# Weight conversions at other steps of the attention, and a combination with one ScalarE copy

## The chip, the cores and the metric

The kernel runs on one core of a Trainium2 chip. The metric is the time of one execution on the device in microseconds; it is the median of three runs. Beside it stands one execution that the hardware profiler recorded, with its trace.

## What is computed

Two batches of eight heads attend over 768 positions, each query only to keys in the same hash bucket. The output, as 1536 rows of 512, goes through two expert layers. All of it is float32; matrix products run as sums of a high and a low part of each operand.

```python
q_bits = (np.einsum('bhsd,dk->bhsk', q, proj) > 0)          # 6 bits; k_bits likewise
mask = q_bucket[:, :, :, None] == k_bucket[:, :, None, :]
scores = np.where(mask, scale * np.matmul(q, k.transpose(0, 1, 3, 2)), -1000000000.0)
attn = np.exp(scores - np.max(scores, axis=-1, keepdims=True))
attn = attn / (np.sum(attn, axis=-1, keepdims=True) + 1e-09)
x = np.matmul(attn, v)                                      # to (1536, 512)
h = x @ w_in; g = np.where(h > 0.0, h, np.exp(np.minimum(h, 0.0)) - 1.0); x = g @ w_out
p = domain_probs / (domain_probs.sum(-1, keepdims=True) + 1e-09)
out = sum(p[:, e:e + 1] * (np.maximum(x @ w1[e], 0.0) @ w2[e]) for e in range(4))
```

The weights `w_in` and `w_out` arrive as 64-bit floats and are turned into 32-bit ones on the chip, by integer and float instructions on their two words.

## The kernel before

**Attention.** The sixteen heads go in eight pairs, each pair in twelve steps: six blocks of 128 queries for each of its two heads. The order on every engine is the order in which the program emits its instructions, and in a step (`att_step`) that is the order of the letters in `ORDER`. C combines a finished product with v (`emit_comb`). E is the exponential of the next block (ScalarE), T and t are transposes of its two halves (TensorE), H and h their high parts copied from PSUM (ScalarE, line 431), Q the scores two blocks ahead (TensorE, lines 385 and 386), N their masked minimum (VectorE, line 395), L and l the low parts (VectorE, line 428), M, m and d the preparation of later pairs, V a third of a product with v. The scores have one buffer, so Q waits for the N before it. The step with index 3 of a pair (5 in pair zero) is the hashing step: twelve more products, whose sign VectorE compares on line 371 and SyncE then moves to the operands.

**The combination.** A product with v has its two parts (with the high and with the low part of v) in the two halves of the partitions. Lines 457 and 458 copy them from PSUM by ScalarE, each 64x384, the second into the first one's partitions, and GpSimd adds them on line 459. It runs at every third step. At steps 3 and 6 GpSimd also normalises half of the pair before (`emit_fin`, line 489) and splits it.

**Weight conversion.** `conv_w` turns one block of 128 hidden units of both weights from 64 to 32 bits. In two halves each: an absolute value by ScalarE (line 248), five steps by VectorE (lines 249, 250, 252, 254, 255) and an addition by GpSimd (line 262). Then `consumed` frees the buffer `raw`, of which there is one until step 83 of 96, and queues the load of the next block on SyncE; `split_w` makes the high and low parts on GpSimd. That is a list of eighteen entries per block, for the blocks 0, 1 and 2. It is worked off one entry at a time at the ends of steps 3, 4, 5, 7, 8 and 9 of pairs one to three (block 0) and four to six (block 1), and one or two per step in pair seven (block 2).

**SyncE's queue.** `loads_step` sends the transfers of the next pair at the ends of steps: the placing of q and k and of their bits, sixteen transfers at steps 2 and 3, and the loads of k at step 2 and of q at step 4 for the pair after.

**Probabilities.** `emit_probs` normalises `domain_probs` after step 10 of pair zero: three additions and three more instructions on VectorE.

After the attention come the expert layers, `TAIL` and then long runs of TensorE products.

Of the kernel before, what the change touches and what calls it, by code (L numbers as in the profile page):

```python
# [7 lines left out]
F32 = mybir.dt.float32  # L8
# [4 lines left out]
ACTF = mybir.ActivationFunctionType  # L13
ALU = mybir.AluOpType
PSUM = bass.MemoryType.PSUM

P = 128
# [18 lines left out]
def lsh_attention_moe_kernel(  # L36
# [14 lines left out]
    nc = tc.nc  # L51
    B, H, S, D = q.shape
# [3 lines left out]
    E = dprobs.shape[1]  # L56
# [3 lines left out]
    HS = S // 2  # L60
# [6 lines left out]
    NPRE = 2  # L67
# [3 lines left out]
    assert len(FT) == DFF // P and GS[0] == NPRE + 1  # L71
    NG = G1 + E
    WA = 3
    ORDER = "CETHQtNLhlMmdV"
    WARM = (9, 2, 5)
    GL = 0.0
    TAIL = "AoqpBpcpproppqppVVVncxkgogkqffzkffppppfffffffffffffffffoqfffffffff"
# [9 lines left out]
    cv_p = ctx.enter_context(tc.tile_pool(name="cv", bufs=1))  # L87
# [7 lines left out]
    l1 = late.enter_context(tc.tile_pool(name="l1", bufs=1))  # L95
# [33 lines left out]
    def split_v(g2, par):  # L129
        if par == 0:  # L130
            vs_t[g2] = l2.tile([P, NJ, 4 * D], F32R, tag="vs", name="vs")
        t = vs_t[g2]
        pool_split(t[:, :, 3 * par * D:(3 * par + 1) * D], t[:, :, (1 + par) * D:(2 + par) * D],
                   raws.pop((g2, par)))
# [12 lines left out]
    dp = l1.tile([P, B * NJ, E], F32, tag="rx", name="dp")  # L147
# [28 lines left out]

    def emit_probs():
        sm = edge_t[:, 0:B * NJ]
        nc.vector.tensor_add(sm, dp[:, :, 0], dp[:, :, 1])
        for e in range(2, E):  # L180
            nc.vector.tensor_add(sm, sm, dp[:, :, e])
        nc.vector.tensor_scalar(out=sm, in0=sm, scalar1=1e-9, scalar2=None, op0=ALU.add)
        nc.vector.reciprocal(out=sm, in_=sm)
        nc.vector.tensor_tensor(out=pn, in0=dp, in1=sm.unsqueeze(2).to_broadcast([P, B * NJ, E]),
                                op=ALU.mult)
# [21 lines left out]
    def consumed(g, m, split):  # L207
        if (not split) if wide and g < G1 else (split and m % 2):
            raw_free.append(raw_used.pop(0))
            loads()  # L210
# [54 lines left out]
    def split_w(g, m, pool, eng, part=None):  # L265
        if part != 1:
            wt[g, m] = pool.tile([P, 4, DM], F32R, tag="w", name="w")
        t = wt[g, m]
        for i, s in enumerate(w32[g, m]):
            if part == 1 - i:  # L270
                continue
            hi, lo = t[:, 2 * i, :], t[:, 2 * i + 1, :]
            if i == 0:
                hi = hi.rearrange("p (c f) -> p c f", f=P)
                lo = lo.rearrange("p (c f) -> p c f", f=P)
            if "p" in eng:
                nc.gpsimd.tensor_scalar(out=hi, in0=s, scalar1=1.0, scalar2=1.0, op0=ALU.mult, op1=ALU.mult)
            else:
                nc.scalar.activation(out=hi, in_=s, func=ACTF.Copy)
            if "P" in eng:  # L280
                nc.gpsimd.tensor_tensor(out=lo, in0=s, in1=hi.bitcast(F32), op=ALU.subtract)
            else:
                nc.vector.tensor_tensor(out=lo, in0=s, in1=hi.bitcast(F32), op=ALU.subtract)
        if part != 0:
            del w32[g, m]
# [3 lines left out]
    NU = NPAIR * 2 * NJ  # L289
    UC = NJ // 2  # L290
# [98 lines left out]
    def emit_min(u):  # L389
        mn = a2.tile([P, 1], F32, tag="mn", name="mn")  # L390
        mn_t[u] = mn
        n = u % (3 + EX) if u < NU - PU - EU else (u + (3 + EX) * PU) % 3
        pool, tag = (a4, f"mk{n}") if n < 3 else (xp, "x" + "hl"[n - 3] + str(NC - 1))
# [53 lines left out]
    def emit_comb(c):  # L447
        g, half = divmod(c, 2)
        g2, par = divmod(g, 2)
        if par == 0 and half == 0:  # L450
            u_t[g2] = l2.tile([P, S], F32, tag="u", name="u")
        ps = pv_t.pop(c)
        del pth_t[c], ptl_t[c]
        o0 = par * D
        t1 = l1.tile([P, HS], F32, tag="t1", name="t1")[o0:o0 + D]
        uu = u_t[g2][o0:o0 + D, half * HS:(half + 1) * HS]
        nc.scalar.activation(out=uu, in_=ps[o0:o0 + D, 0:HS], func=ACTF.Copy)
        nc.scalar.activation(out=t1, in_=ps[D - o0:2 * D - o0, 0:HS], func=ACTF.Copy)
        nc.gpsimd.tensor_tensor(out=uu, in0=uu, in1=t1, op=ALU.add)

    def emit_rinv(g2):
        sm = sums_t[g2]
# [38 lines left out]
            nc.tensor.transpose(ps[:, i * P:(i + 1) * P], rx_t[g2][:, half * UC + i].rearrange("p h d -> p (h d)"), ident)  # L501

    PU = 2 * NJ
    M_AT = (0, 1, 2, 3, 10, 11)
    PLACE_AT = (2, 3, 3, 11)
    V_AT = (8, 9)
# [2 lines left out]
    LE, LN, LQ = 1, 2, 2  # L509
    EX = 0  # L510
    EU = 0
    PRE_EVERY = 3
    LASTN = (1, 2, 2, 1, 2, 1, 2, 2, 2, 1, 1, 1)
    FIN_AT = (3, 6)
    PRE_AT = (3, 4, 5, 7, 8, 9)
    MSTEP = [None] * PU
    for i, st in zip(M_AT, (("n",), ("t", "q", 0), ("t", "q", UC), ("h",), ("t", "k", 0), ("t", "k", UC))):
        MSTEP[i] = st
# [14 lines left out]
    def loads_step(g2, i):  # L533
        if g2 + 2 < NPAIR and i in L_AT:
            load_qk(g2 + 2, "kq"[L_AT.index(i)])
        if g2 + 1 < NPAIR:
            q0, b0, kq1, _ = (4, 5, 5, 0) if g2 == 0 else PLACE_AT
            if g2 == 0 and i == 1:
                place(g2 + 1, "k", 0)
            if i == q0:  # L540
                place(g2 + 1, "q", 0)
            if i == b0:
                for nm in "kq":
                    place_bits(g2 + 1, nm, 0)
            if i == kq1:
                for nm in "kq":
                    place(g2 + 1, nm, 1)
                    place_bits(g2 + 1, nm, 1)
        if i == PLACE_AT[3] and g2 + 2 < NPAIR:
            place(g2 + 2, "k", 0)  # L550
        if i in FIN_AT and 0 < g2 < NPAIR:
            half = FIN_AT.index(i)
            emit_fin(g2 - 1, half, rx_t[g2 - 1][:, half * HS:(half + 1) * HS])
        if g2 + 1 < NPAIR and i < 2:
            load_v(g2 + 1, i)
        if g2 + 1 < NPAIR and i in V_AT:
            split_v(g2 + 1, V_AT.index(i))

    def run(stages):
        for f in stages:  # L560
# [68 lines left out]
    for par in range(2):  # L629
        split_v(0, par)  # L630
    nc.sync.dma_start(out=dp.rearrange("p (b j) e -> p b j e", b=B),
                      in_=dprobs.rearrange("(b p j) e -> p b j e", b=B, j=NJ))
# [4 lines left out]
            emit_min(u)  # L637
    for u in range(LE):
        emit_exp(u)
    pre, done = [], []  # L640

    def att_step(u):
        g2, i = divmod(u, PU)
        v = u - LT
        c, part = divmod(v, UC)
        mc[0] = c - 1
        ops = {}
        if u + LQ < NU:
            ops["Q"] = lambda: emit_qk(u + LQ)
        if u + LN < NU:  # L650
            ops["N"] = lambda: emit_min(u + LN)
        if u + LE < NU:
            ops["E"] = lambda: emit_exp(u + LE)
        if done:
            ops["C"] = lambda: emit_comb(done.pop())
        if 0 <= v < NU:
            for h in range(2):
                ops["Tt"[h]] = lambda h=h: emit_t(v, h)
                ops["Hh"[h]] = lambda h=h: emit_parts(v, h, False)
                ops["Ll"[h]] = lambda h=h: emit_parts(v, h, True)  # L660
        if 1 <= c <= NU // UC:
            ops["V"] = lambda: emit_pv(c - 1, part)
        if 1 <= g2 < NPAIR and i == 0:
            emit_rinv(g2 - 1)
        table = MSTEP if g2 else MSTEP0 + [x if x and x[:2] == ("t", "k") else None for x in MSTEP[6:]]
        if g2 == NPAIR - 1:
            table = MSTEP[:1] + [None] * (PU - 1)
        for nm, f in zip("Mmd", prep_step(g2, table[i], u < len(MSTEP0)) if g2 < NPAIR and table[i] else ()):
            if f:
                ops[nm] = f  # L670
        for nm in ORDER:
            if nm in ops:
                ops.pop(nm)()
        assert not ops
        if 1 <= c <= NU // UC and part == UC - 1:
            done.append(c - 1)
        loads_step(g2, i)
        m, k_ = divmod(g2 - 1, PRE_EVERY)
        if g2 >= 1 and m <= NPRE and u < NU:
            if i == 0 and k_ == 0:  # L680
                pre[:] = conv_w(0, m, cv_p, 2) + [lambda: consumed(0, m, False)]
                pre.extend(lambda n=n: split_w(0, m, wpool(m), "pP", n) for n in range(2))
                pre.append(lambda: consumed(0, m, True))
            for _ in range(i in PRE_AT if m < NPRE else LASTN[i]):
                if pre:
                    pre.pop(0)()


    pools, acc, last_x = {}, {}, []
# [103 lines left out]
    def wpool(m):  # L793
        return wa_p if m < NPRE else pools["wb" if m > NPRE else "wm"]
# [11 lines left out]
    def l1_step(n):  # L806
# [7 lines left out]
        first, *rest = l1_out(*x, l1_mm(*x))  # L814
        first()
        return rest

    def take(fill, n):
        for f in fill[:n]:
            f()  # L820
        del fill[:n]

    def new_conv():

# [405 lines left out]
    fin, outq = [], []  # L1230
    for u in range(NU - 2):
        att_step(u)
        if u == PU - 2:
            emit_probs()
        if u == NU - PU - 1:
            early.close()
            for i in range(2):
                raw_free.append(open_pool(f"raw{i + 2}", 1, "right"))
            open_pool("wm", 1, "right")
            loads()  # L1240
        if u == NU - PU + 6:
            l1_start(0)
        take(parts, 1)
# [13 lines left out]
    for n in range(GS[0] + 2, len(seq) + LAG):  # L1257
        if ahead[0][0] == G1 and "hf" not in pools:
            open2()
        rest = l1_step(n)  # L1260
# [35 lines left out]
```

## Time and profile before

| | us |
|---|---|
| median of three runs | 1027.78 (1027.49 to 1028.94) |
| the profiled execution | 1028.59 |
| its span, first to last instruction | 1026.8 |
| attention, first to last step | 15.3 to about 256 |
| TensorE busy in the span | 1009.4 |
| VectorE, ScalarE, GpSimd busy | 833.6, 519.1, 493.6 |

The page gives busy time per engine and the costliest groups of instructions; the trace answers for single lines, stretches and the order of time. A busy TensorE isn't one at its peak, as the ends of its products are modelled, so lengths of steps are read from the starts of the transposes on line 414.

### The profile page before, as it was taken

Reading aid. Unit: us, or ns where it says so; the run is one execution under the profiler, and the core shown is the slowest. Engines: PE = TensorE matmul, PEld = TensorE weight load, DVE = VectorE, ACT = ScalarE, POOL = GpSimd, SP = SyncE. Lnnn points to the kernel's source line nnn. Section 1 sums busy time; section 2 is a strip of 40 time slices with the busy share of each in tenths; the row PEclk is TensorE's granted clock in tenths of the full one; section 3 lists DMA queues with packets and bytes.
Section 4 is the critical chain, followed back from the end, with each engine's and each line's share of the span. In section 5 each row is a group of like instructions: output and inputs, shape, how many; then the busy total and the mean of one; then the engine's idle time right before and its main releaser. Section 6 shows DMA issues by size and latency. Waiting matters only on the chain.

```text
span 1026.8 us, 16094 instructions
## 1 busy us (share of the span) xinstructions
PE 1009.4 (98%) x5898; PEld 887.8 (86%) x5898; DVE 833.6 (81%) x1283; ACT 519.1 (51%) x1020; POOL 493.6 (48%) x422
## 2 busy tenths in 40 slices
PE   7999999999999999999999999999999999999998
PEld 5898999898877888888789999999999999999997
DVE  6788888988778888624558778999999998999994
ACT  5898899898566455435433323333243333333331
POOL 2566676575356455522321243454635455465442
PEclk9999999999999999999999999999999999999999
DMA  6856576471122222100020020020300202011012
GB/s 156 191 137 147 136 176 146 111 222 58 41 82 82 83 82 82 42 1 22 1 92 1 1 98 17 1 82 1 103 11 1 83 11 93 11 38 46 1 41 82
DMA packets 72709, 72.23 MB, mean 70 GB/s; under 512 B 26148, under 2 KB 60664, under 8 KB 72632
## 3 DMA queue, kind: packets, MB, share of 16 engines
q1 hardware_dynamic: 72328, 71.14, 24.7%
q8 instruction: 47, 0.77, 0.3%
q14 instruction: 30, 0.25, 0.1%
q10 hardware_dynamic: 304, 0.07, 0.1%
HBM read 48.98 MB, written 3.21 MB: 51 GB/s over the span
## 4 chain that ended last, share of the span: by engine, by line
PE 50%; issue 6%; POOL 2%; DVE 0%; POOLq 0%
PE l L1024 22%; PE a L972 4%; PE r L972 4%; PE r L971 4%; PE a L971 4%; PE a L973 4%; PE r L973 4%; POOL h L752 2%; PE l L1130 1%; PE l L768 1%; PE r L716 0%; PE r L715 0%; PE r L714 0%; DVE a L1138 0%; DVE op L910 0%
## 5 line engine op out<-in xcount | busy, mean ns | idle before, releaser
L1024 PEld LDWEIGHTS l<-w,op 128*128 128x128 f32 x1932 | 240.9, 188 | 7.1
L1024 PE MATMUL l<-w,op 128*128 128x256 f32 x1932 | 242.8, 280 | 0.0
L1040 POOL TENSOR_TENSOR a<-a,temps 128x512 f32<-128x512 f32 x60 | 91.6, 1527 | 120.6 <-DVE a L1035 118.8
L768 PE MATMUL l<-h,w 128*128 128x512 f32 x576 | 140.3, 391 | 1.5 <-POOL h L752 1.4
L906 ACT ACTIVATE op<-hf 128x512 fp32r<-128x512 f32 x119 | 73.1, 626 | 135.2 <-DVE hf L976 84.4
L752 POOL TENSOR_TENSOR h<-g,h 128x512 fp32r<-128x512 f32 x44 | 70.0, 1591 | 132.1 <-ACT h L748 87.3
L768 PEld LDWEIGHTS l<-h,w 128*128 128x128 f32 x576 | 107.4, 188 | 26.6 <-POOL h L752 3.6
L910 DVE TENSOR_TENSOR op<-hf,op 128x512 fp32r<-128x512 f32 x119 | 126.4, 1076 | 4.9 <-ACT op L906 4.8
L395 DVE TENSOR_SCALAR_CACHE_REDUCE mk<-s 128x768 f32<-128x768 f32 x96 | 91.4, 952 | 22.1 <-PE s L386 19.3
L428 DVE TENSOR_TENSOR ptl<-pt,pth 128x384 fp32r<-128x384 f32 x192 | 97.7, 550 | 11.0 <-ACT pth L431 10.9
L414 PE MATMUL pt<-cst,mk 128*128 128x128 f32 x576 | 94.8, 274 | 0.6 <-ACT mk L404 0.4
L404 ACT ACTIVATE mk<-mk,mn 128x768 f32<-128x768 f32 x96 | 89.7, 935 | 10.8 <-DVE mk L395 10.3
L431 ACT ACTIVATE pth<-pt 128x384 fp32r<-128x384 f32 x192 | 83.8, 481 | 8.3 <-PE pt L414 8.0
L385 PE MATMUL s<-ks,qs 128*128 128x512 f32 x192 | 80.3, 440 | 7.6 <-DVE mk L395 7.3
L414 PEld LDWEIGHTS pt<-cst,mk 128*128 128x128 f32 x576 | 71.1, 140 | 12.7 <-ACT mk L404 5.3
L972 PE MATMUL a<-xl,w 128*128 128x512 f32 x192 | 75.1, 391 | 0.0
L972 PE MATMUL r<-xl,w 128*128 128x512 f32 x192 | 75.0, 391 | 0.0
L971 PE MATMUL a<-xh,w 128*128 128x512 f32 x192 | 75.0, 391 | 0.0
L971 PE MATMUL r<-xh,w 128*128 128x512 f32 x192 | 75.0, 390 | 0.0
L973 PE MATMUL a<-xh,w 128*128 128x512 f32 x192 | 74.7, 389 | 0.0
L973 PE MATMUL r<-xh,w 128*128 128x512 f32 x192 | 74.7, 389 | 0.0
L444 PE MATMUL pv<-pth,vs 128*128 128x384 f32 x192 | 72.1, 375 | 0.0
(159 smaller groups left out, 2149.8 us busy)
## 6 DMA issues: line engine op xcount, KB each, us to landing
raw<-in_moe_w_dram SPq DMA_DIRECT2D x32, 512.0 KB
raw<-in_moe_w_in_dram SPq DMA_DIRECT2D x16, 512.0 KB
raw<-in_moe_w_out_dram SPq DMA_DIRECT2D x16, 512.0 KB
ks<-kh SPq DMA_DIRECT2D x15, 384.0 KB
qs<-qh SPq DMA_DIRECT2D x30, 192.0 KB
sk<-in_k_dram SPq DMA_DIRECT2D x8, 384.0 KB
sq<-in_q_dram SPq DMA_DIRECT2D x8, 384.0 KB
ks<-kl SPq DMA_DIRECT2D x16, 192.0 KB
```

Of the source, the lines that this page charges most:

```text
L395: nc.vector.tensor_scalar(out=e_t[u], in0=s_t.pop(u)[:, 0:S], scalar1=MASKED, scalar2=None, op0=ALU.min, op1=ALU.min, accum_out=mn)
L404: nc.scalar.activation(out=e, in_=e, func=ACTF.Exp, bias=mn_t.pop(u), scale=-1.0, accum_out=sums_t[g2][:, j, par:par + 1])
L414: nc.tensor.transpose(pt[:, i * P:(i + 1) * P], e_t[u][:, kb * P:(kb + 1) * P], ident)
L428: nc.vector.tensor_tensor(out=lo, in0=pt, in1=hi.bitcast(F32), op=ALU.subtract)
L752: eng.tensor_tensor(out=hl[:, cs], in0=gt[:, cs], in1=hh[:, cs].bitcast(F32), op=ALU.subtract)
L768: mm(ps, a, b_, start=(m == 0 and n == 0), stop=(m == GS[g] - 1 and n == 2))
L910: e.tensor_tensor(out=lo, in0=x, in1=hi.bitcast(F32), op=ALU.subtract)
L971: mm(ps, wh[:, cs], xh[c][:, ts], start=(c == 0), stop=False)
L972: mm(ps, wh[:, cs], xl[c][:, ts], start=False, stop=False)
L973: mm(ps, wl[:, cs], xh[c][:, ts], start=False, stop=(c == NC - 1))
L1024: mm(ps[:, tt * HD:(tt + 1) * HD], a[:, cs], b_[:, k_], start=(n == 0), stop=(n == 11))
L1040: nc.gpsimd.tensor_tensor(out=x, in0=x, in1=keep[nm], op=ALU.add)
```

## The change

It touches four things.

- The conversion entries stand at steps that a table names. A block begins in an even pair (`k_` 0: steps 8 and 10), goes on in the next (`k_` 1: steps 1, 2, 3 and 10) and ends in the one after (`k_` 2: steps 0, 3, 4, 5 and 6). Block 0 begins in pair zero, block 1 in pair two, block 2 in pair four; block 2 leaves its splits to pair seven (`k_` 3: steps 2 and 4). Three entries stand at each hashing step, in the order of the step as the letter W, between l and M. So pairs two and four end one block and begin the next.
- A combination copies all 128 partitions by one ScalarE instruction, GpSimd moves the half that lies in the other partitions and then adds. The last two combinations keep two ScalarE copies.
- The probabilities stand at step 5 of pair zero as W, with one reduction for the three additions.
- The first half of the normalisation goes from step 3 to step 4.

```diff
-    ORDER = "CETHQtNLhlMmdV"
+    ORDER = "CETHQtNLhlWMmdV"
...
-        nc.vector.tensor_add(sm, dp[:, :, 0], dp[:, :, 1])
-        for e in range(2, E):
-            nc.vector.tensor_add(sm, sm, dp[:, :, e])
+        nc.vector.tensor_reduce(out=sm, in_=dp, axis=mybir.AxisListType.X, op=ALU.add)
...
-        nc.scalar.activation(out=uu, in_=ps[o0:o0 + D, 0:HS], func=ACTF.Copy)
-        nc.scalar.activation(out=t1, in_=ps[D - o0:2 * D - o0, 0:HS], func=ACTF.Copy)
-        nc.gpsimd.tensor_tensor(out=uu, in0=uu, in1=t1, op=ALU.add)
+        here, there = slice(o0, o0 + D), slice(D - o0, 2 * D - o0)
+        if c < NU // UC - 2:
+            nc.scalar.activation(out=t1, in_=ps[:, 0:HS], func=ACTF.Copy)
+            nc.gpsimd.tensor_copy(uu, t1[there])
+        else:
+            nc.scalar.activation(out=t1[here], in_=ps[here, 0:HS], func=ACTF.Copy)
+            nc.scalar.activation(out=uu, in_=ps[there, 0:HS], func=ACTF.Copy)
+        nc.gpsimd.tensor_tensor(out=uu, in0=uu, in1=t1[here], op=ALU.add)
...
-    FIN_AT = (3, 6)
-    PRE_AT = (3, 4, 5, 7, 8, 9)
+    FIN_AT = (4, 6)
+    PRE = {(0, 8): 1, (1, 1): 1, (0, 10): 1, (1, 2): 1, (1, 3): 3, (1, 10): 1, (2, 0): 1, (2, 3): 3, (2, 4): 3, (2, 5): 1,
+           (2, 6): 2, (3, 2): 1, (3, 4): 2}
...
+    def pre_step(g2, i):
+        for k_ in (3, 2, 1, 0):
+            m = (g2 - k_) // 2
+            if (g2 - k_) % 2 == 0 and 0 <= m <= NPRE and (k_, i) in PRE and not (m == NPRE and k_ == 2 and i > 4):
+                if m not in pre:
+                    a, b_, t0, t1, *rest = conv_w(0, m, cv_p, 2)
+                    pre[m] = [a, t0, b_, t1] + rest + [lambda: consumed(0, m, False)]
+                    pre[m].extend(lambda n=n: split_w(0, m, wpool(m), "pP", n) for n in range(2))
+                    pre[m].append(lambda: consumed(0, m, True))
+                take(pre[m], PRE[k_, i])
...
+        if u < NU and i == 3:
+            ops["W"] = lambda: pre_step(g2, 3)
+        if u == PROBS_AT:
+            ops["W"] = emit_probs
...
-        m, k_ = divmod(g2 - 1, PRE_EVERY)
-        if g2 >= 1 and m <= NPRE and u < NU:
...
+        if u < NU and i != 3:
+            pre_step(g2, i)
...
-        if u == PU - 2:
-            emit_probs()
```

## Rows read from the trace of the kernel before

**Rows 1.** The page, part 1: busy us and share of each engine.

```profile
PE 1009.4 (98%) x5898; PEld 887.8 (86%) x5898; DVE 833.6 (81%) x1283; ACT 519.1 (51%) x1020; POOL 493.6 (48%) x422
```

**Rows 2.** Pairs one to seven: length; busy PE, PEld, DVE, ACT, POOL; clock, DMA, GB/s.

```profile
45.74:76.79 31.05, 29.42 (x194) 26.80 (x193) 27.05 (x61) 28.22 (x64) 18.40 (x22) 1.00 0.60 141
76.79:108.07 31.28, 29.62 (x195) 26.96 (x194) 28.47 (x58) 26.94 (x62) 19.26 (x22) 1.00 0.57 132
108.07:136.96 28.89, 28.89 (x194) 26.69 (x193) 23.85 (x52) 26.40 (x62) 23.33 (x27) 1.00 0.73 178
136.96:166.23 29.27, 29.17 (x195) 26.73 (x194) 25.33 (x56) 27.68 (x64) 19.43 (x24) 1.00 0.62 141
166.23:197.50 31.27, 29.61 (x195) 26.96 (x194) 28.49 (x58) 26.93 (x62) 19.01 (x22) 1.00 0.58 133
197.50:225.86 28.36, 28.36 (x188) 26.09 (x187) 23.52 (x50) 25.86 (x60) 22.79 (x26) 1.00 0.67 171
225.86:255.98 30.12, 28.91 (x178) 25.00 (x177) 26.93 (x59) 26.15 (x58) 16.13 (x17) 1.00 0.30 103
```

**Rows 3.** Timeline, hashing step of pair three: start, length, engine, line.

```profile
118.28 1.02 POOL L489 TENSOR_TENSOR u<-u,rx 128x384 f32<-128x384 f32 x1 [0.23 <-DMA rx<-d]
...
117.85 1.02 DVE L428 TENSOR_TENSOR ptl<-pt,pth 128x384 fp32r<-128x384 f32 x2 [0.46 <-ACT pth L431]
118.88 0.68 DVE L371 TENSOR_SCALAR hb<-m,cst 128x384 fp32r<-128x384 f32 x1
120.61 0.96 DVE L395 TENSOR_SCALAR_CACHE_REDUCE mk<-s 128x768 f32<-128x768 f32 x1 [1.06 <-PE s L386]
```

**Rows 4.** Timeline of TensorE at the start of pair one.

```profile
47.44 0.50 PE L385 MATMUL s<-ks,qs 128*128 128x512 f32 x1 [1.21 <-DVE mk L395]
```

**Rows 5.** Two source lines: times each, shortest, median and longest ns.

```profile
L457 ACT ACTIVATE u<-pv x32: 483/485/489, 32.5 to 262.9; 64x384 f32<-64x384 f32 x32
...
L588 POOL COPY s<-sq x1: 504/504/504, 5.6 to 5.6; 128x384 f32<-128x384 f32 x1
```

**Rows 6.** Source lines of the conversion in the attention.

```profile
L248 ACT ACTIVATE w<-raw x6: 653/674/680, 57.6 to 231.1; 128x512 f32<-128x512 f32 x6
...
L249 DVE TENSOR_SCALAR w<-w x6: 415/417/419, 64.0 to 234.1; 128x512 f32<-128x512 f32 x6
...
L255 DVE SCALAR_TENSOR_TENSOR raw<-raw x6: 675/678/1535, 101.0 to 247.9; 128x512 f32<-128x512 uint32 x6
```

**Rows 7.** Timeline, where a conversion step and GpSimd meet in pair two.

```profile
101.02 1.53 DVE L255 SCALAR_TENSOR_TENSOR raw<-raw 128x512 f32<-128x512 uint32 x1
...
101.98 0.94 POOL L137 TENSOR_SCALAR vs<-sv 128x384 fp32r<-128x384 f32 x1
```

**Rows 8.** Timeline of SyncE's queue in pair three, first bits and load.

```profile
119.93 1.97 SPq L356 DMA_DIRECT2D ks<-hb  x2
...
131.34 0.78 SPq L224 DMA_DIRECT2D raw<-in_moe_w_in_dram  x1
```

**Rows 9.** Stretches of one us behind that load; columns as in rows 2.

```profile
135.00:136.00 1.00, 1.00 (x9) 0.92 (x8) 0.65 (x2) 1.00 (x4) 0.92 (x2) 1.00 1.04 382
136.00:137.00 1.00, 1.00 (x9) 0.97 (x8) 1.00 (x3) 1.00 (x3) 0.98 (x2) 1.00 0.55 221
137.00:138.00 1.00, 1.00 (x9) 0.91 (x7) 1.00 (x3) 0.90 (x3) 0.94 (x1) 1.00 0.03 12
```

**Rows 10.** Timeline of ScalarE and TensorE, steps 8 to 10 of pair three.

```profile
129.10 0.85 ACT L431 ACTIVATE pth<-pt 128x384 fp32r<-128x384 f32 x2
...
131.06 0.93 ACT L404 ACTIVATE mk<-mk,mn 128x768 f32<-128x768 f32 x1
...
132.13 0.55 PE L414 MATMUL pt<-cst,mk 128*128 128x128 f32 x3
```

**Rows 11.** Timeline of TensorE's first products, 128x512 each.

```profile
1.31 3.54 PE L572 MATMUL pz<-z 128*128 128x512 bf16 x9 [1.31 <-POOL z L567]
...
10.85 1.25 PE L572 MATMUL pz<-z 128*128 128x512 bf16 x5
```

More of the change, by code (lines that the diff above doesn't have):

```diff
@@ L454, in emit_comb @@
         o0 = par * D
-        t1 = l1.tile([P, HS], F32, tag="t1", name="t1")[o0:o0 + D]
+        t1 = l1.tile([P, HS], F32, tag="t1", name="t1")
         uu = u_t[g2][o0:o0 + D, half * HS:(half + 1) * HS]
-        nc.scalar.activation(out=uu, in_=ps[o0:o0 + D, 0:HS], func=ACTF.Copy)
-        nc.scalar.activation(out=t1, in_=ps[D - o0:2 * D - o0, 0:HS], func=ACTF.Copy)
-        nc.gpsimd.tensor_tensor(out=uu, in0=uu, in1=t1, op=ALU.add)
+        here, there = slice(o0, o0 + D), slice(D - o0, 2 * D - o0)
[6 more added lines that the diff above has]
+        nc.gpsimd.tensor_tensor(out=uu, in0=uu, in1=t1[here], op=ALU.add)
     def emit_rinv(g2):
@@ L503, in lsh_attention_moe_kernel @@
     PU = 2 * NJ
+    PROBS_AT = 5
     M_AT = (0, 1, 2, 3, 10, 11)
@@ L511, in lsh_attention_moe_kernel @@
     EU = 0
-    PRE_EVERY = 3
-    LASTN = (1, 2, 2, 1, 2, 1, 2, 2, 2, 1, 1, 1)
-    FIN_AT = (3, 6)
-    PRE_AT = (3, 4, 5, 7, 8, 9)
+    FIN_AT = (4, 6)
+    PRE = {(0, 8): 1, (1, 1): 1, (0, 10): 1, (1, 2): 1, (1, 3): 3, (1, 10): 1, (2, 0): 1, (2, 3): 3, (2, 4): 3, (2, 5): 1,
+           (2, 6): 2, (3, 2): 1, (3, 4): 2}
     MSTEP = [None] * PU
@@ L557, in loads_step, with take @@
             split_v(g2 + 1, V_AT.index(i))
+    def take(fill, n):
+        for f in fill[:n]:
+            f()
+        del fill[:n]
     def run(stages):
@@ L639, in lsh_attention_moe_kernel @@
         emit_exp(u)
-    pre, done = [], []
+    pre, done = {}, []
+    def pre_step(g2, i):
[8 more added lines that the diff above has]
+                take(pre[m], PRE[k_, i])
     def att_step(u):
@@ L677, in att_step @@
         loads_step(g2, i)
-        m, k_ = divmod(g2 - 1, PRE_EVERY)
-        if g2 >= 1 and m <= NPRE and u < NU:
[L680 to L686, printed above, removed]
+        if u < NU and i != 3:
+            pre_step(g2, i)
     pools, acc, last_x = {}, {}, []
@@ L816, in l1_step @@
         return rest
[L818 to L821, printed above, removed]
     def new_conv():
```

## The prediction

> **What bounds the kernel now.** The page's busy shares come first [rows 1]: TensorE works in 98% of the span, so from the expert layers on (about 256 us) there is nothing for this edit to win, and whatever the attention gains or loses arrives at the end unchanged. Next I cut the attention into its eight pairs, twelve steps each, at the first transpose of each pair [rows 2]; pair zero, not shown there, runs from 15.33 to 45.74. In pair three VectorE converts no weights and TensorE leaves no gap: 28.89 us. It is my floor. Pairs two and five, with six conversion instructions on VectorE each, take 31.28 and 31.27; pair four, with four cheaper ones and two on ScalarE, 29.27; pair one, with the same six and the probabilities at its start, 31.05. In those the reader sees VectorE, not TensorE, near its limit: 28.47 of 31.28 against 23.85 of 28.89. One step breaks the rule: in the hashing step TensorE has twelve products more, and VectorE then waits 1.06 us for the next scores [rows 3]. That is the cover the change aims at. The third view is SyncE's queue, because a weight conversion reads `raw`, and `raw` is one buffer until step 83: its next load goes out only behind everything queued there.
>
> **The template.** I work inside pair three, on the trace's own clock. Its hashing step: low parts done at 118.87, comparison 118.88 to 119.56, next minimum at 120.61 [rows 3].
>
> **Conversions leave their old places.** Pairs one, two, four and five go back to the floor before new costs: 31.05, 31.28, 29.27 and 31.27 all become 28.89. The probabilities' part of pair one is the wait of 1.21 us that TensorE shows for a minimum queued behind six small VectorE instructions [rows 4], with what follows from it. In pair seven a whole conversion but for its splits goes. The same one cost 0.38 in pair four and 2.38 in pair five, 2.76 together; pair seven has steps with expert products, where TensorE is longer, so I take 2.4 (1.5 to 3.5): 30.12 becomes 27.7.
>
> **Probabilities at step 5.** Step 5 of pair zero is its hashing step; four instructions in place of six, under 1 us, fit into the 1.06 us: nothing, 0.3 if that cover is gone.
>
> **The combination.** ScalarE issues one copy of 0.48 us less [rows 5] every third step. TensorE is at its floor in pair three, so only the wait for an exponential behind the two copies can come back: 0.2 per pair (0 to 0.4). GpSimd gains a copy of 64x384 to other partitions. No row has a copy across partitions; a straight 128x384 one takes 0.50 [rows 5], the multiplication behind it 1.02 [rows 3]; below zero is excluded, it is an added instruction. I take 0.5, as the nearest kind. Four per pair add 2 us to a queue busy 23.33 in pair three, which holds the additions and splits that pairs two and four now get: 25.3 of 28.89 [rows 2]. GpSimd still fits. The last two combinations keep their count. Moving the normalisation from step 3 to 4 changes nothing: GpSimd's order (combination, then normalisation) stays.
>
> **Conversions at the hashing step.** With the shorter combination VectorE is through with the low parts about 0.45 earlier, near 118.4. Odd pairs put two one-input steps and one two-input step there, 0.42 + 0.42 + 0.68 = 1.52 [rows 6]; even pairs 0.42 + 0.68 + 0.68 = 1.78. The comparison (0.68) is queued behind them, SyncE's bit transfers and the next minimum behind it. Undisturbed, the comparison ends at 120.6 (odd) or 120.9 (even), so the minimum of 120.61 is 0 or 0.3 late. But GpSimd is busy just then, with a multiplication at 118.28 and two splits after it. When a conversion met GpSimd at 101.02 it took 1.53 in place of 0.68, and GpSimd's next, a 0.51 instruction, 0.94 [rows 6, 7]: one waits for the other. If the engines alternate, a multiplication of 1.02 and a split of 0.51 slip in: 1.5 more. I take the middle: 0.8 in odd pairs (0 to 1.5), 1.1 in pair six (0.3 to 1.8). The Trainium skill ("SBUF — State Buffer", section "SBUF: two separate sides") calls the port that the two share an exclusive lock, held for the whole instruction, the loser blocked; it names no order among waiters, so by it the sum may stand at either end. Single conversions at steps 0, 1, 2 and 10 (0.42 to 0.68) meet about 0.4 us of spare VectorE time per step (5.04 over twelve): 0.4 per odd pair, 0.2 in pair six, 0.3 in pair zero, which gets 0.2 back.
>
> **The load behind the second and third conversion.** This decides. In pair two the additions at step 4 free `raw`; only then is the load of the next weight queued on SyncE, and the first conversion step of that weight, on ScalarE, stands at step 8 of the same pair. Pair four does so again for the third weight. In the kernel before, the same load was queued at step 5 of pair three, behind the same transfers: SyncE started on the bits at 119.93 and on `raw` at 131.34, 11.4 us of issuing one transfer after another [rows 8]. Traffic ends in the microsecond after 136, at 12 GB/s after it [rows 9]; half a megabyte is 1.4 us at those rates, so the first half was there between 135.2 and 137.0. I take 136.0. No one waited for it, since its conversion stood in pair four. After the change ScalarE reaches it when step 8's copies are done, 129.95 [rows 10], and holds the queue: the combination, the exponential that step 10 transposes and all copies stand behind. After landing come the absolute value (0.67), the combination (about 0.4 of issue) and the exponential (0.93), 2.0 together; then step 10's transposes, which stood at 132.13 [rows 6, 10]. The comparison now ends 1.3 (undisturbed) to 2.8 later than 119.56 and the whole SyncE chain with it: I take 2.1. So 136.0 + 2.0 + 2.1 = 140.1, against 132.13: **8.0 us** per pair (6.4 to 9.7). The hashing step's own cost is swallowed by this.
>
> TensorE then stands for some 8 us, longer than in any row of before; its granted clock is 1.00 in all pairs [rows 2]. What follows an idle stretch is seen at the start alone: the first nine products took 3.54 us, 0.39 each, near the lower level of 1.2 GHz, five later ones 1.25, 0.25 each [rows 11]. Nine at the later price would have taken 2.25, so the slow start cost 1.3. I take 1.3 after each stall (0 to 3). The Trainium skill ("TensorE: Matmul & The Clock Gate", Part 1) says the same of an idle array, that it falls to half its rate; if it did not here, the sum would be 2.6 less. Pairs two and four: 28.89 + 8.0 + 1.3 - 0.1 = 38.1.
>
> **The sum.** Pair zero +0.1; one 28.89 + 0.8 + 0.4 - 0.2 = 29.9, -1.15; two 38.1, +6.8; three 29.9, +1.0; four 38.1, +8.8; five 29.9, -1.4; six 28.36 + 1.1 + 0.2 - 0.2 = 29.5, +1.1; seven -2.4. Together **+12.8**. The profiled execution took 1028.59, its span 1026.8; it becomes 1041.4. The median of the runs, 1027.78, becomes **1040.6**.
>
> **Rivals.**
> 1. *The load is there in time.* Then pairs two and four cost 28.89 + 1.1 + 0.3 - 0.2 = 30.1 and the sum is -3.2: 1024.6; with an undisturbed VectorE in the hashing steps -8, 1019.8. It decides if SyncE reaches the load 6 us sooner than before. Against it: nothing in the change shortens that queue, and the bits start later. For it: only a transfer order that I misread. 0.13.
> 2. *The engines alternate in the hashing steps.* 0.7 more in pairs one, three, five and six, 0.7 more on each stall: +4.2, 1044.8. For it: rows 7; against it: one meeting, not three in a row. 0.15.
> 3. *The stall without a slower clock.* 1038.0. For it: the stretch has work until step 9 and the clock never fell before. 0.20.
> Between them, gains at their best and stalls at their shortest, 28.89 + 6.4 in pairs two and four and the low ends elsewhere, give +1: about no change, 0.03.
>
> **How the numbers follow.** Forecast 0.49, rivals 0.13, 0.15, 0.20, the rest 0.03. All but the first rival and that rest are slower. Low 1028 is the shortest stall with the best gains, high 1048 the alternation with the longest loads; what is left out is the first rival and a little beyond 1048. Some 0.2% is what a measurement tells from no change: faster 0.13, within 0.03, slower 0.84.
>
> **What would show it.** In the trace after: ScalarE idle 6 us or more before line 248's first instruction in pairs two and four, released by a DMA into `raw`; pairs near 38 us there and near 30 in one, three, five; the granted clock below 1.00 just behind each; line 255 stretched at hashing steps; pair seven near 27.7. Wrong would be a ScalarE that finds `raw` landed at step 8, or a floor that pair three does not set.

## The result, and the profile after

| | before | after |
|---|---|---|
| median of six runs, us | 1027.74 | 1041.88 (1040.21 to 1043.97) |
| ratio | | 1.0133 [1.0116, 1.015] |
| the profiled execution | 1028.59 | 1042.87 |
| its span | 1026.8 | 1041.1 |
| the eight pairs together | 240.65 | 254.83 |

The change makes the kernel 1.3% slower; 1040.6 had been forecast, within 1028 to 1048. The eight pairs lost 14.2 us and the span 14.3: what the attention loses arrives at the end unchanged. Of all executions below one was far off, 2584 us with the new combination alone, and no ratio counts it. The page's first part, to be read against [rows 1]: ScalarE is busy 16 us less, GpSimd 15 us more, and the kernel is slower all the same.

```profile
PE 1012.6 (97%) x5898; PEld 896.3 (86%) x5898; DVE 838.7 (81%) x1281; ACT 503.1 (48%) x990; POOL 508.5 (49%) x452
```

The windows of after, pairs zero to seven, answer to [rows 2]; after the stretch come its length, busy time of PE, PEld, DVE, ACT and POOL, the granted clock, DMA share and GB/s.

```profile
15.32:46.45 31.13, 30.78 (x187) 28.14 (x188) 24.92 (x55) 24.91 (x57) 15.06 (x20) 0.89 0.86 204
46.45:75.88 29.43, 28.61 (x194) 26.90 (x193) 27.46 (x57) 24.87 (x59) 21.08 (x26) 1.00 0.61 140
75.88:115.80 39.92, 31.76 (x194) 29.49 (x193) 27.36 (x57) 25.43 (x59) 27.26 (x32) 0.87 0.53 130
115.80:145.25 29.45, 28.63 (x194) 26.91 (x193) 27.45 (x57) 24.89 (x59) 21.09 (x26) 1.00 0.60 140
145.25:184.57 39.32, 31.38 (x195) 29.20 (x194) 27.09 (x57) 25.46 (x59) 27.13 (x32) 0.87 0.53 132
184.57:213.99 29.42, 28.60 (x194) 26.91 (x193) 27.44 (x57) 24.84 (x59) 21.06 (x26) 1.00 0.61 141
213.99:242.45 28.46, 27.96 (x188) 26.26 (x187) 26.33 (x54) 23.89 (x56) 21.86 (x26) 1.00 0.61 157
242.45:270.15 27.70, 27.39 (x178) 25.17 (x177) 22.22 (x49) 23.24 (x52) 14.88 (x18) 1.00 0.26 88
```

Two pairs, two and four, take 39.9 and 39.3 in place of 31.28 and 29.27 [rows 2]: 18.7 us lost. Pairs one, five and seven gain 5.9 together. The other pairs move by 0.7 or less. In the two long pairs alone behind the start the clock is below 1.00, and TensorE is busy 8 us less than the pair lasts. Where they lose it, the timeline of ScalarE in pair two shows (start, length, engine, line; in brackets the idle time ahead and what ended it):

```profile
97.54 0.90 ACT L429 ACTIVATE pth<-pt 128x384 fp32r<-128x384 f32 x2
106.05 0.66 ACT L246 ACTIVATE w<-raw 128x512 f32<-128x512 f32 x1 [7.61 <-DMA raw<-in_moe_w_in_dram]
106.61 0.47 ACT L457 ACTIVATE t<-pv 128x384 f32<-128x384 f32 x1
106.98 0.93 ACT L402 ACTIVATE mk<-mk,mn 128x768 f32<-128x768 f32 x1
```

Line 246 is the absolute value (248 before), 457 the combination's copy, 402 the exponential. ScalarE stands 7.61 us before the second conversion's first entry, with the combination and the next exponential queued behind it. SyncE's queue shows why, in the same pair, as in [rows 8]:

```profile
89.50 1.61 SPq L354 DMA_DIRECT2D ks<-hb  x2
...
99.75 0.69 SPq L117 DMA_DIRECT2D sq<-in_q_dram  x1
100.55 0.78 SPq L222 DMA_DIRECT2D raw<-in_moe_w_in_dram  x1
```

From the first bits at 89.50 to the load at 100.55 are 11.05 us of issuing; [rows 8] had 11.4. ScalarE was ready at 98.4, 2.1 us before the load was even issued, and the wait ended 5.5 us after the issue. TensorE hangs on that exponential:

```profile
100.35 0.34 PE L443 MATMUL pv<-ptl,vs 128*128 128x384 f32 x1
108.05 0.90 PE L412 MATMUL pt<-cst,mk 128*128 128x128 f32 x3 [7.36 <-ACT mk L402]
```

And behind the gap the clock is low. The windows of steps 8, 9, 10 and 11 of that pair, columns as above, and step 10 of pair three last:

```profile
96.39:98.45 2.06, 2.06 (x15) 1.95 (x14) 1.89 (x5) 1.83 (x4) 1.89 (x3) 1.00 0.74 169
98.45:108.05 9.60, 2.24 (x15) 1.82 (x13) 2.03 (x6) 2.00 (x5) 4.18 (x7) 0.79 0.71 194
108.05:112.59 4.54, 4.54 (x17) 4.25 (x18) 3.25 (x7) 3.53 (x8) 2.68 (x4) 0.50 0.00 0
112.59:115.80 3.21, 3.21 (x18) 2.99 (x17) 1.15 (x3) 1.67 (x5) 1.28 (x2) 0.73 0.00 0
140.47:142.86 2.39, 2.39 (x18) 2.27 (x17) 2.22 (x7) 2.39 (x7) 1.92 (x3) 1.00 0.74 170
```

Steps 10 and 11 take 2.40 and 2.39 in pair three of the same trace. Here they take 4.54 and 3.21 with the same products: 2.14 + 0.82 = 3.0 us lost. TensorE is 100% busy in both; only the clock column shows the loss.

### The profile page after: what moved, and what is told of

Read it like the earlier page. It is cut to its first block, busy times and chain, and to the rows that moved or that the text cites. A ratio compares the mean times of both kernels' runs of the same rounds, so it can differ in the third digit from the quotient of the medians.

```text
span 1041.1 us, 16127 instructions
## 1 busy us (share of the span) xinstructions
PE 1012.6 (97%) x5898; PEld 896.3 (86%) x5898; DVE 838.7 (81%) x1281; ACT 503.1 (48%) x990; POOL 508.5 (49%) x452
## 3 DMA queue, kind: packets, MB, share of 16 engines
HBM read 48.98 MB, written 3.21 MB: 50 GB/s over the span
## 4 chain that ended last, share of the span: by engine, by line
PE 50%; issue 6%; POOL 2%; DVE 0%; POOLq 0%
PE l L1035 22%; PE a L983 4%; PE r L983 4%; PE a L982 4%; PE r L982 4%; PE r L984 4%; PE a L984 4%; POOL h L768 2%; PE l L1141 1%; PE l L784 1%; PE r L731 0%; PE r L730 0%; PE r L732 0%; DVE a L1149 0%; DVE op L921 0%
## 5 line engine op out<-in xcount | busy, mean ns | idle before, releaser
L768 POOL TENSOR_TENSOR h<-g,h 128x512 fp32r<-128x512 f32 x44 | 66.4, 1508 | 134.2 <-ACT h L764 89.2
L412 PE MATMUL pt<-cst,mk 128*128 128x128 f32 x576 | 97.7, 280 | 15.0 <-ACT mk L402 14.8
L412 PEld LDWEIGHTS pt<-cst,mk 128*128 128x128 f32 x576 | 74.9, 145 | 24.5 <-ACT mk L402 16.5
L383 PE MATMUL s<-ks,qs 128*128 128x512 f32 x192 | 82.9, 453 | 5.6 <-DVE mk L393 5.5
```

Source lines behind the costliest of these rows:

```text
L412: nc.tensor.transpose(pt[:, i * P:(i + 1) * P], e_t[u][:, kb * P:(kb + 1) * P], ident)
L768: eng.tensor_tensor(out=hl[:, cs], in0=gt[:, cs], in1=hh[:, cs].bitcast(F32), op=ALU.subtract)
```

## The experiments

The length of a step is the distance between the first transposes (line 412) of one step and the next, as in the prediction. Conversions that hold VectorE up in the hashing step, index 3, are seen in the length of step 5: there TensorE waits for the minimum queued behind them. Differences between kernels of different batches go by their ratios to the kernel before, of which 0.001 is 1.03 us. The theory: the load behind `raw` makes the two stalls, and they alone make the kernel slower.

**The first entries in the pair after.** The load stays where it is; each block's first two entries stand at step 0 of the odd pair, where the first conversion step finds its weight long there. The first block moves with the others, to pair one.

```diff
-    PRE = {(0, 8): 1, (1, 1): 1, (0, 10): 1, (1, 2): 1, (1, 3): 3, ...
+    PRE = {(1, 0): 2, (1, 1): 1, (1, 2): 1, (1, 3): 3, ...
```

> Edit: each block's conversion begins at step 0 of the pair after (absolute values and first limit there) and no longer at steps 8 and 10 of the pair in which its load is queued; all else as in the kernel after. Theory (ScalarE waits for the load): its two waits for a DMA into raw, 7.6 and 7.7 us, are gone, the granted clock stays 1.00 behind pairs two and four, these pairs take 29 to 30 us in place of 39.9 and 39.3, and the time falls by two stalls of 7.5 and some 5 us of half-speed steps: 1041.9 - 20 = about 1022, between 1019 and 1025. Rival (ending one block and beginning the next in one pair is too much for GpSimd or VectorE there): the work only moves on, pairs two and four stay above 33 and the time above 1030.

Measured: 1021.22, ratio 0.9925 [0.9907, 0.9942]; pairs 30.22, 31.07, 29.43, 29.04, 29.14, 28.79, 28.78, 27.68. No wait of ScalarE for `raw` is left, and pair two reads:

```profile
76.09:105.51 29.42, 28.62 (x194) 26.91 (x193) 26.95 (x56) 24.58 (x58) 25.52 (x30) 1.00 0.68 166
```

The same conversion work stands in the same pairs, but for two entries, and the clock is back at 1.00. Pairs two and four give back 20.7 us together, which is all of the loss and more: without the stalls the change is a gain of 0.75%. Pair one rose from 29.43 to 31.07 with the first block's entries; why they cost more there than in pairs three and five wasn't looked into.

**The load through another queue.** Nothing in the table changes; the two loads in question go out from GpSimd instead of SyncE.

```diff
+        eng = nc.gpsimd if g == 0 and m in (1, 2) else nc.sync
-        nc.sync.dma_start(out=t1 ...
+        eng.dma_start(out=t1 ...
```

> Edit: the loads of blocks 1 and 2 are issued from GpSimd's queue, right behind the additions that free the buffer; the conversion steps stay where the kernel after has them. Theory (the load is late because SyncE issues 13 transfers before it): the load starts 5 us or more sooner, ScalarE's wait falls from 7.6 us to under 3, and the time to 1022 to 1031. Rival (the load is late by itself: additions that end late, or a slow transfer): ScalarE still waits over 5 us in pairs two and four and the time stays above 1036.

Measured: 1033.85, ratio 1.0053 [1.0036, 1.0071], between the theory's 1022 to 1031 and the rival's 1036. Timeline of GpSimd and ScalarE in pair two (each line stands one higher here, 247 is the absolute value):

```profile
91.76 0.97 POOL L223 DMA_DIRECT2D raw<-in_moe_w_in_dram  x1 [0.31 <-POOL w L261]
...
100.30 1.26 POOL L280 TENSOR_TENSOR w<-w,w 128x512 fp32r<-128x512 f32 x1
...
101.59 0.67 ACT L247 ACTIVATE w<-raw 128x512 f32<-128x512 f32 x1 [3.98 <-POOL w L280]
```

The same split in after, line 279 there:

```profile
99.21 1.28 POOL L279 TENSOR_TENSOR w<-w,w 128x512 fp32r<-128x512 f32 x1
```

Counted from the pair's first step (75.08 here, 75.88 in after), the load is issued 8.0 us sooner, and the DMA no longer ends ScalarE's wait. But ScalarE still waits 3.98 us here and 5.4 in pair four, now for the split of the weight before it, on line 280, which reads the one buffer `w` that the absolute value writes. So the queue was the last of two waits; the one behind it is 2 to 4 us shorter as measured here, and moving the load alone can't bring the whole gain. Part of it is the edit's own: the two issues stand on GpSimd ahead of the splits, which end 26.5 us into pair two in place of 24.6, 1.9 us later, and 2.0 later in pair four. In after the splits would have held ScalarE for some 2.1 and 2.7 us had the load been there, an estimate from their ends and the times at which ScalarE was ready.

**The load ahead of the q load, with the additions ahead of the normalisation.** At step 4 the conversion's entries run before `loads_step`.

```diff
+        if u < NU and i == 4:
+            pre_step(g2, i)
...
-        if u < NU and i != 3:
+        if u < NU and i not in (3, 4):
```

> Edit: at step 4 the load into raw is queued on SyncE ahead of the load of q, which was one place before it. Theory (SyncE's order sets the landing): one transfer less in front, 0.8 us of issue, and its traffic behind in place of ahead; ScalarE's two waits shrink by 0.8 to 2 us each, from 7.6 to 5.6 to 6.8, and the time by 1.5 to 4, to 1038 to 1040.5. Rival (the additions, not the queue, set the start): the waits stay within 0.3 us of 7.6.

Measured: 1035.37, ratio 1.0063 [1.0045, 1.0082], 7.2 us under after. The waits of ScalarE (total us, times, longest) come down from 15.3 by 2.6 only:

```profile
ACT w L246 <- DMA raw<-in_moe_w_in_dram: 12.7, 2, 7.2
```

The rest was not expected: step 5 of pairs two, four and six, 3.14, 2.81 and 2.83 in after, is 2.06 here, at the floor. Two things stood together in this edit, the load's place on SyncE and GpSimd's order, so it doesn't tell them apart.

**The load's place on SyncE alone.** Only the q load moves behind the entries of step 4; GpSimd's order is that of after.

```diff
-        if g2 + 2 < NPAIR and i in L_AT:
+        if g2 + 2 < NPAIR and i in L_AT and i != 4:
...
+        if g2 + 2 < NPAIR and i == 4:
+            load_qk(g2 + 2, "q")
```

> At step 4 the load into raw is queued on SyncE ahead of the load of q, as in the earlier kernel with the load first, but GpSimd keeps the order of the kernel after (normalisation, then additions). Theory (two effects stood together there: SyncE's order and GpSimd's): the hashing step of the even pairs stays stretched, step 5 at 2.8 to 3.15 us, and only the two waits for the load shrink by 0.8 to 2 us each: 1038 to 1040.5. Rival (the order on SyncE was all of it): 1034 to 1036 again, and step 5 of the even pairs at 2.07 us.

Measured: 1037.46, ratio 1.0082 [1.0065, 1.0099], 5.2 us under after. The waits:

```profile
ACT w L246 <- DMA raw<-in_moe_w_in_dram: 11.3, 2, 5.8
```

Each wait is some 2.0 us shorter, the slower clock behind them costs 2.3 and 1.5 in place of 3.0 and 2.6, and step 5 of the even pairs stays at 2.81 to 3.13. In pair two the load is issued at 98.92, by the start of the hashing step 0.7 us sooner than in after, and lands 4.1 us later in place of 5.5, with the q load's bytes no longer ahead of it. The time is a little under the 1038 to 1040.5 that the theory had. So the short step 5 of the experiment before comes from GpSimd's order, and what stands ahead of the load on SyncE goes into the stall twice, by its issue and by its transfer.

**The normalisation away from the hashing step.** If a conversion step is stretched because GpSimd works beside it, taking GpSimd's work away must bring step 5 to its floor.

```diff
-    FIN_AT = (4, 6)
+    FIN_AT = (6, 9)
```

> Edit: the two halves of the normalisation on GpSimd are queued behind the combinations of steps 6 and 9, in place of steps 4 and 6, so that GpSimd has nothing but the combination to do while VectorE converts in the hashing step. Theory (VectorE and GpSimd exclude each other, and GpSimd's instructions slip in between the conversions): lines 248, 250 and 253 shorten toward 0.42 and 0.68 us at the hashing steps, step 5 of the odd pairs falls from 3.15 us to 2.3 to 2.7, and the time by 2 to 5 us, to 1037 to 1040. Rival (the conversions' own 1.5 to 1.8 us are what VectorE cannot place): step 5 stays at 3.0 or more and the time within 1 us of 1041.9.

Measured: 1041.76, ratio 1.0129 [1.0107, 1.015], no better than after, where the theory had 1037 to 1040. The mechanism is there all the same. First VectorE in the hashing step of pair three in after, then the same in this kernel (248 and 250 are conversion steps, `x2` two in a row; 369 is the comparison):

```profile
125.82 2.09 DVE L248 TENSOR_SCALAR w<-w 128x512 int32<-128x512 int32 x2
127.83 0.98 DVE L250 SCALAR_TENSOR_TENSOR w<-raw,w 128x512 int32<-128x512 int32 x1
128.74 0.66 DVE L369 TENSOR_SCALAR hb<-m,cst 128x384 fp32r<-128x384 f32 x1
```

```profile
126.69 1.28 DVE L248 TENSOR_SCALAR w<-w 128x512 int32<-128x512 int32 x2
127.89 0.68 DVE L250 SCALAR_TENSOR_TENSOR w<-raw,w 128x512 int32<-128x512 int32 x1
128.49 0.67 DVE L369 TENSOR_SCALAR hb<-m,cst 128x384 fp32r<-128x384 f32 x1
```

Beside the first stood GpSimd's queue, in after:

```profile
125.47 1.01 POOL L462 TENSOR_TENSOR u<-u,t 64x384 f32<-64x384 f32 x1
126.56 1.07 POOL L492 TENSOR_TENSOR u<-u,rx 128x384 f32<-128x384 f32 x1
127.72 0.57 POOL L137 TENSOR_SCALAR xh<-u 128x384 fp32r<-128x384 f32 x1
```

Beside the second only the addition on line 462. Step 5 of pairs three and five falls from 3.15 to 2.06. The conversion entries there cost nothing of themselves. Two things ate the gain. The two waits grew to 19.7 together: ScalarE, through with a shorter step 5, only waits longer for a load that still sets the end, and SyncE reached that load 2.2 us later in pair two, 0.4 in pair four, for a reason that is open. And pair seven rose by 2.3, since its first expert products need the normalised rows that now come at step 9.

```profile
ACT w L246 <- DMA raw<-in_moe_w_in_dram: 19.7, 2, 10.8
```

**The combination alone, and all but the combination.** The first is the kernel before with the new combination and nothing else of the change, the second the change with the old combination; their diff is that of `emit_comb` above, done and undone.

> The kernel before with the new combination alone (one ScalarE copy of 128 partitions, GpSimd moves the half and adds). The prediction's term: 0.2 us per pair, 1026 to 1026.5 beside 1028. Theory after the result (steps 5 to 9 of every pair came down to 2.07 us, so the second copy had held all of them): 0.36 per pair and some more in steps 0 and 3, 1024.5 to 1026. Rival (GpSimd's extra 0.5 us copy, at every third step, meets VectorE's conversions and takes the gain back): 1027.5 to 1029.

> The kernel after with the old combination (two ScalarE copies, no shift on GpSimd); all else stays. Theory (the combination gains 0.36 us per undisturbed pair, and its missing copy lets VectorE into the hashing step 0.45 us sooner): pairs one, three, five, six and seven 0.5 to 0.9 us longer, the stalls of pairs two and four as they are: 1044 to 1046. Rival (GpSimd's copy costs in the hashing step as much as ScalarE's saves): 1041 to 1043.

Measured: alone 1024.17, ratio 0.9956 [0.994, 0.9972], a gain of 4.5 us; undone 1052.51, ratio 1.0223 [1.0196, 1.0251], 9.2 us over after, and so are its eight pairs, 263.99 against 254.83. The first is a little beyond what was expected, the second far beyond. For the first, VectorE at step 7 of pair three, behind a combination, in the kernel before and then with the combination alone (428 are the low parts):

```profile
126.18 1.02 DVE L428 TENSOR_TENSOR ptl<-pt,pth 128x384 fp32r<-128x384 f32 x2 [0.46 <-ACT pth L431]
```

```profile
123.47 1.02 DVE L428 TENSOR_TENSOR ptl<-pt,pth 128x384 fp32r<-128x384 f32 x2
```

With two copies ScalarE comes late with the high parts and VectorE waits 0.46 us, four times in the pair; with one copy it doesn't. Pair three falls from 28.89 to 28.36, though TensorE's record was solid in both:

```profile
106.06:134.42 28.36, 28.36 (x195) 26.88 (x194) 23.79 (x52) 24.52 (x58) 24.11 (x30) 1.00 0.71 174
```

Undone, the loss lies mostly at three steps: step 0 of pairs two, four and six 3.05 to 3.08 against 2.18, step 3 of the odd pairs 4.60 to 4.64 against 4.19, step 5 3.57 to 3.84 against 2.81 to 3.16. At step 0 of pair six, with the old combination, the two copies (455, 456) stand ahead of the exponential, and TensorE waits for it:

```profile
220.56 0.49 ACT L455 ACTIVATE u<-pv 64x384 f32<-64x384 f32 x1
221.07 0.48 ACT L456 ACTIVATE t<-pv 64x384 f32<-64x384 f32 x1
221.57 0.94 ACT L402 ACTIVATE mk<-mk,mn 128x768 f32<-128x768 f32 x1
...
222.59 0.27 PE L469 MATMUL m<-cst,sums 128*12 128x128 f32 x1 [0.71 <-ACT mk L402]
```

The waits for `raw` stay at 15.2 (7.4 and 7.8), so the combination and the stalls are separate.

**The probabilities alone.** The kernel before with `emit_probs` at step 5 of pair zero and its one reduction.

> The kernel before with the probabilities alone moved to the hashing step of pair zero, with one reduction. Theory: the wait of 1.21 us at the start of pair one goes and step 0 of pair one falls from 4.14 us to 2.3: 1.2 to 1.9 us less, 1026 to 1027. Rival (what was queued behind them is late anyway): within 0.3 us of before.

Measured: 1026.28, ratio 0.9978 [0.9964, 0.9991]. Pair one falls from 31.05 to 29.25, its step 0 from 4.14 to 2.30: the wait of [rows 4] was most of it.

**Both findings together.** Block 0 keeps its places; blocks 1 and 2 begin at step 0 of the odd pair; the normalisation stands at steps 6 and 9 but in the last pair, whose products need it sooner.

```diff
+    PRE0 = {...}
+    PRE = {**PRE0, (1, 0): 2}
+    del PRE[0, 8], PRE[0, 10]
...
+            tab = PRE0 if m == 0 else PRE
...
+        fin_at = FIN_AT if g2 == NPAIR - 1 else (6, 9)
```

(`PRE0` is the table of the change.)

> The kernel after with two edits: blocks 1 and 2 begin at step 0 of the pair after their load is queued (block 0 begins in pair zero as before), and the normalisation stands behind the combinations of steps 6 and 9, but for the last pair. Theory (the load and the exclusion of VectorE and GpSimd are all that the change lost): no wait of ScalarE for a DMA, no step 5 above 2.4 us, pairs one to six at 27.7 to 28.9: 1013 to 1018. Rival (GpSimd, moved later, holds the next pair's parts or the splits): gains on the first kernel with later conversions, 1021.2, of under 1 us.

Measured: 1016.86 (1016.35 to 1017.01), ratio 0.9873 [0.9851, 0.9895], faster than both kernels: 1.3% under the kernel before, 2.6% under the change. Pairs two and four are at the floor that the combination alone had shown, 28.36, with the conversions in them:

```profile
73.55:101.91 28.36, 28.36 (x194) 26.90 (x193) 26.12 (x56) 24.53 (x58) 25.63 (x31) 1.00 0.60 141
131.61:159.97 28.36, 28.36 (x195) 26.89 (x194) 26.12 (x56) 24.54 (x58) 25.63 (x31) 1.00 0.63 148
```

VectorE is busy 26.12 of 28.36 there: the steps have room for the conversions. Not all came as expected: pairs one, three and five take 29.27, 29.69 and 29.05, above the 28.9 expected at most; step 5 is 2.56 and 2.60 in pairs one and five, above 2.4; and one wait for `raw` of 0.7 us is left, in pair three.

## Why the prediction came out right, and which of its terms did not

| pair | forecast | measured | measured, by its steps |
|---|---|---|---|
| zero | 30.5 | 31.13 | 30.41, as with the q load moved, plus 0.7 of slow clock at the start |
| one | 29.9 | 29.43 | floor 28.36 + 1.08 |
| two | 38.1 | 39.92 | 28.36 + 1.08 + 7.54 + 2.96 |
| three | 29.9 | 29.45 | 28.36 + 1.09 |
| four | 38.1 | 39.32 | 28.36 + 0.75 + 7.63 + 2.58 |
| five | 29.9 | 29.42 | 28.36 + 1.08 |
| six | 29.5 | 28.46 | 27.71 + 0.76 |
| seven | 27.7 | 27.70 | |

The floors are those of pairs three and six with the combination alone. In the last column the first term behind the floor is the hashing step's (what step 5 has above 2.07), then the wait in step 9, then the clock. The eight forecasts sum to 253.6, the pairs to 254.83.

- **The load behind the second and third conversion.** Right in kind, place and size: SyncE's queue decides, ScalarE holds everything behind the absolute value, and pair two's step 10 begins 1.08 + 7.54 = 8.6 us late, pair four's 0.75 + 7.63 = 8.4, where 8.0 (6.4 to 9.7) had been worked out. The time of step 10 within pair two came out within 0.2 us, 32.17 for 32.03, by errors that nearly cancel: the bits began 1.8 later in the pair for the 2.1 taken, the queue took 11.05 for 11.4 [rows 8], the landing 5.5 for 4.7, and what stands behind it 2.0 as taken. The entries moved to the pair after show that the load is the cause. What the step didn't see is the split behind it, on the buffer `w`: it costs nothing while the load is later, and an estimated 2 to 3 us in this kernel were the load in time.
- **The clock.** Right in kind, mis-sized: 1.3 per stall (0 to 3), from the nine products of [rows 11], against 3.0 and 2.6 here. The granted clock stood at 0.50, which is the 1.2 GHz level, over a whole step, and at 0.73 over the next. The Trainium skill's rule that an idle array falls to half its rate ("TensorE: Matmul & The Clock Gate", Part 1) agrees with that 0.50. The rival without a slower clock falls. So does the row as a measure: [rows 11] has nine products, 3.5 us of TensorE's first work; here the clock stayed at 0.50 for 6.3 and 5.4 us of products, and a little under half of that is the loss.
- **The hashing step.** Right in size: 1.1 in odd pairs for 0.8 (0 to 1.5), 0.76 in pair six for 1.1 (0.3 to 1.8). Two steps of 0.42 took 2.09 and one of 0.68 took 0.98: 1.55 too much in sum, as much as the alternation's 1.5, of which 1.1 reached the length of the step. With the normalisation gone, 1.28 and 0.68, nothing of it did. So the engines do take turns, as the second rival had it, but its price was too high: a cover that the forecast had put at nothing hid some 0.45 us, the 1.55 less the 1.1. The Trainium skill ("SBUF — State Buffer", section "SBUF: two separate sides") has the lock held for a whole instruction; the trace agrees, and for the order that it leaves open these durations fit one instruction of each in turn.
- **The single conversions.** Forecast 0.4 per odd pair, measured nothing: steps 0, 1, 2 and 10 of pair three are 2.18, 2.40, 2.39 and 2.40, just as in pair three of the combination alone, which has no conversions. An entry of 0.42 to 0.68 against a mean of 0.42 spare per step was counted as a loss; no step grew by it.
- **The combination.** Mis-sized: 0.2 per pair (0 to 0.4) where it gave 0.53. The failed sentence is that TensorE is at its floor in pair three: a record without gaps was read as one that can't shrink. The steps with a combination held a wait of VectorE for the high parts. On GpSimd the step was right: its copy takes 0.499 us for the 0.5 that were taken, as this source line shows (shortest, median, longest ns):

```profile
L458 POOL COPY u<-t x30: 498/499/503, 34.1 to 264.0; 64x384 f32<-64x384 f32 x30
```

- **The probabilities and pair seven.** Right: alone the first gives 2.3 us, and pair one drops by 1.8; the hashing step of pair zero hides them. Pair seven is at 27.70. One reading there was wrong without a consequence: pair one of before has four conversion instructions on VectorE and two on ScalarE, like pair four, and not the six of pair two; what it took above pair four's 29.27 is the 1.8 of the probabilities.

The clock cost 2.9 us more than forecast, the two delays of step 10 together 1.0, the start 0.6; the floor of pairs two and four was 0.9 less, and the combination, the single conversions and the hashing steps came out 2.4 less in the four undisturbed pairs (29.9, 29.9, 29.9 and 29.5 against 29.43, 29.45, 29.42 and 28.46). The eight pairs missed by 1.2 only, and so close partly by luck, because these errors had opposite signs; the sign and the size of the loss come from the stall, which was right by itself.

## What to carry to other kernels

Before an operation is moved to an earlier place, find the last of what it reads, and when that is issued on an in-order queue: a load that no one waited for yesterday is on the path as soon as its reader stands first. When such a wait is taken away, look for the next one on the same operands, which a shorter queue uncovers. And a busy engine without gaps in its record isn't proof of a floor; the length of a step against the same step in another pair, or with one load taken off, is.

## What the runs showed of the hardware

- **A stall costs more than its length, by how long the clock stays low behind it.** By steps 10 and 11 against 2.39 to 2.45 undisturbed, the slower clock cost 1.7 after ScalarE's waits of 4.0 and 5.4 us (the load through another queue), 1.5 to 2.5 after 5.4 to 5.8 and 2.9 after 7.2 (the load ahead of the q load, both ways), 3.0 and 2.6 after 7.6 and 7.7 (after), but 1.9 and 1.7 after 7.4 and 7.8 (the old combination), and 2.4 and 2.5 after 10.8 and 8.9 (the normalisation moved). So the length of the wait doesn't set it. In all twelve the loss is 0.46 to 0.49 of the time for which the clock still stood at 0.50 once TensorE had begun again: 6.3 us in pair two of after, shown here, 3.1 in the shortest. What sets that time is not settled.

```profile
108.05:114.35 6.30, 6.30 (x24) 5.82 (x25) 3.25 (x7) 4.38 (x10) 3.97 (x5) 0.50 0.00 0
```

- **The clock can fall at the start too.** In the profiled execution of after it was granted at 0.51 from 15.32 to 22.25, and pair zero's first two steps took 3.78 and 3.15; with the q load moved, the kernel does the same work in that pair and its first steps took 2.52 and 2.12. Pair zero was 0.7 us longer for it. The mean clock of that execution is 0.987, of the five others 0.990, so the start's share may be its own. The profiled executions of three experiments have it too (the first entries in the pair after, the normalisation moved, the old combination). What sets it off was not looked into.

```profile
15.32:22.25 6.93, 6.76 (x26) 5.98 (x27) 3.94 (x9) 4.02 (x9) 0.08 (x1) 0.51 0.73 173
```

- **Twice the partitions cost ScalarE nothing more, and crossing them showed no price on GpSimd.** A ScalarE copy of 128x384 took 0.49 us, the median of 30, where one of 64x384 takes 0.485 [rows 5], so two half copies cost twice one whole. GpSimd's copy of 64x384 to other partitions took 0.499, as much as a straight one of 128x384, 0.504 [rows 5]; no straight one of 64x384 stands beside it.
